# Loading order in a fused linear-attention and expert kernel: reciprocals read back in two halves, wo loaded inside the loop, x tiles on other queues

## The chip, the cores and the metric

The kernel runs on one core of a Trainium2 chip. The core has five engines that run side by side and wait for each other through semaphores: TensorE (PE, with its weight loads PEld), VectorE (DVE), ScalarE (ACT), GpSimd (POOL) and SyncE (SP). SP only issues DMAs here; ScalarE and GpSimd issue a few too. The metric is device time in microseconds (us) for one execution. The kernel before takes 110.32 us, the median of 3 runs (109.84 to 110.73).

## The reference

The input x is one sequence of S = 2048 tokens of D = 640. It is normalised to xn, and three things are added: x, a linear attention of 32 heads on xn, and a small expert block on xn that changes 8 tokens only.

```python
def _A_ref(x, wqkv, wo):                       # on xn
    qkv = (x @ wqkv) ...                       # q, k, v in 32 heads of 20
    phi = lambda t: jnp.where(t > 0, t + 1, jnp.exp(t)) + 1e-6
    pq, pk = phi(q), phi(k)
    kv = jnp.einsum("bhsd,bhse->bhde", pk, v)
    z = jnp.einsum("bhsd->bhd", pk)
    num = jnp.einsum("bhqd,bhde->bhqe", pq, kv)
    den = jnp.einsum("bhqd,bhd->bhq", pq, z)[..., None] + 1e-6
    return (num / den) ... @ wo

def _B_ref(x, w_r, w_gate, w_up, w_down):      # on xn
    r = x @ w_r
    idx = jnp.argsort(-r, axis=-1)[:, :8]      # 8 tokens
    y = (silu(x_sel @ w_gate) * (x_sel @ w_up)) @ w_down * sigmoid(r_sel)
    return x + scatter_add(y at idx)

xn = layernorm(x)
return x + _A_ref(xn, A_wqkv, A_wo) + _B_ref(xn, ...)
```

All inputs and the output are bf16.

## The kernel before

**Tiles.** The tokens are 16 tiles of 128 (T = 16); D is five chunks of 128 (KC = 5, the index m or kc). Everything stays in the core's memory: x_sb and xn hold tokens in rows, xnT, pqT and rb hold features in rows and tokens in columns.

**Order.** The order of the instructions on each engine is written out by hand (manual_schedule); each engine works through its own list strictly in that order. Waits between engines are put in by the framework. DMAs take eight completion semaphores in turn, and a DMA that takes one over waits until the DMA that had it before has landed. SP's DMAs therefore stand in one queue, in program order, and a DMA that waits holds up those behind it.

**Start (lines 108 to 118).** SP and ScalarE read x tiles, wk (the k columns of wqkv, in two parts: chunks 0 to 2 and 3 to 4) and wq. Tile 0 comes in two halves of 320 columns, tile 1 whole on SP (L111), tile 2 on SP (L114), tile 3 on ScalarE (L115), tiles 4 to 7 in one DMA on SP (L118). VectorE takes the statistics of each tile (ln_stats, L165), GpSimd the root, VectorE normalises (ln_norm, L193). The first three tiles are transposed on TensorE, later ones by a DMA transpose on SP (L198) into xnT.

**Loop over tiles (L437 to L471).** For tile t, TensorE multiplies k (L240, needs xnT of t), the Gram matrix of xn with phi(k) of tile t - 1 (ga_mm, L263, tiles gaC and gaD) and q (L252). ScalarE and VectorE turn q and k into phi(q) = pqT and phi(k) = pk. In each round late_loads(t) lets SP issue one of the remaining loads: x tiles 8 to 15, wg, wu, wd and wv, by a table. From t = 12 keep(...) copies x + xn to a scratch in DRAM (xcp, L390).

**Between loop and output.** Column sums of pk go through zpart and four tiny DMAs (zrel, L522) to give z; late_loads(16) then loads wo, in two DMAs (L380, L381). TensorE goes on with the Gram matrix (gb1, L533; gb2, L630), multiplies the denominators (pden, L611), and the gate and up projections of the 8 tokens (L643). ScalarE takes the reciprocals as exp(-ln den), rden, laid out as 4 groups of 32 heads by 512 tokens.

**Reciprocals (L656 to L683).** rden has heads in rows, but pqT has features in rows. So four stores on SP (rscr_store, one for each 512 tokens) write it to a DRAM scratch rscr, and rb_load(a, b) reads tokens a to b back, each head's row spread over its features: five DMAs, one for each m. The first call takes SP and ScalarE in turn, the others SP alone. norm(a, b) on VectorE then multiplies pqT by rb for tiles a to b; norm(0, 2) needs the five DMAs that bring tokens 0 to 511, norm(8, 12) and norm(12, 16) those of the last 1024 tokens.

**Output.** GT, the whole Gram matrix, times wv gives kvT (L708, L715), kvT times wo gives M in five chunks (m_chunk, L743; copied out by ScalarE and once by VectorE, L754). In VectorE's list stand, in this order: kvT, norm(0, 2), y_sb (the copy of the 8 tokens' result py, L774), M's chunk 3, norm(2, 4), norm(4, 8), norm(8, 12), norm(12, 16), the additions. M's chunk 4 is multiplied into the same buffer that py had. y_sb is scattered onto xcp by GpSimd (L775), and x_sb is read back from there (L780). o_mm(t) (L795) multiplies pqT by M for tile t; x_sb is added, and the tile is written out.

Of the kernel before, what the change touches and what calls it, by code (L numbers as in the profile page):

```python
# [9 lines left out]
S = 2048  # L10
D = 640
# [3 lines left out]
T = S // P  # L15
KC = D // P
FC = F // P
C = 8
TBLK = 512
NTB = S // TBLK  # L20
HW = 320
# [4 lines left out]
E0 = (0, 80, 180, 280, 380, 480, 512)  # L26
# [21 lines left out]
def kernel(  # L48
# [13 lines left out]
    nc = tc.nc  # L62
# [4 lines left out]
    x_v = A_x[0].rearrange("(t p) d -> p t d", p=P)  # L67
# [8 lines left out]
    def sb(shape, dt, name, tag=None):  # L76
        return big.tile(shape, dt, tag=tag or name, name=name)
# [7 lines left out]
    x_sb = sb([P, T, D], BF16, "x_sb")  # L85
# [6 lines left out]
    wv = sb([P, KC, D], BF16, "wv")  # L92
    wo = sb([P, NW, D], BF16, "wo")
# [14 lines left out]
    nc.gpsimd.dma_start(wrow[:], B_w_r.rearrange("(kc p) -> kc p", p=P))  # L108
    nc.sync.dma_start(x_sb[:, 0, 0:HW], x_v[:, 0, 0:HW])
    nc.scalar.dma_start(x_sb[:, 0, HW:D], x_v[:, 0, HW:D])  # L110
    nc.sync.dma_start(x_sb[:, 1, :], x_v[:, 1, :])  # L111
    nc.scalar.dma_start(wk[:, 0:3, 0:D], wqkv_v[:, 0:3, D : 2 * D])
    nc.sync.dma_start(wk[:, 3:KC, 0:D], wqkv_v[:, 3:KC, D : 2 * D])
    nc.sync.dma_start(x_sb[:, 2, :], x_v[:, 2, :])  # L114
    nc.scalar.dma_start(x_sb[:, 3, :], x_v[:, 3, :])  # L115
    for a, b in ((0, 3), (3, KC)):
        nc.sync.dma_start(wq[:, a:b, :], wqkv_v[:, a:b, 0:D])
    nc.sync.dma_start(x_sb[:, 4:8, :], x_v[:, 4:8, :])  # L118


    zero = sb([P, P], BF16, "zero")
# [236 lines left out]
    def wo_rows(a, stride, n):  # L358
        return bass.AP(
            tensor=A_wo.tensor, offset=A_wo.offset + a * D,  # L360
            ap=[[D, P], [stride * D, n], [1, D]],
        )

    def late_loads(t):
        def part(dst, src, a, b):
            nc.sync.dma_start(dst[:, a:b, :], src[:, a:b, :])

        wv_v = wqkv_v[:, :, 2 * D : 3 * D]
        plan = {
            2: (x_sb, x_v, 8, 12), 4: (wg, kcF, 0, 1), 5: (x_sb, x_v, 12, 16),  # L370
            6: (wg, kcF, 1, 3), 7: (wg, kcF, 3, 5), 8: (wu, kcU, 0, 2), 9: (wu, kcU, 2, 4),
            10: (wu, kcU, 4, 5), 11: (wd, kcD, 3, 8), 12: (wd, kcD, 8, FC), 13: (wv, wv_v, 0, 2),
            14: (wv, wv_v, 2, KC),
        }
        if t in plan:
            part(*plan[t])
        if t == 10:
            part(wd, kcD, 0, 3)
        if t == 16:
            nc.sync.dma_start(wo[:, 0::6, :], wo_rows(E0[0], E0[6], 2))  # L380
            nc.sync.dma_start(wo[:, 1:6, :], wo_rows(E0[1], 100, 5))  # L381

    gaC = pair("C", "gaC")
    gaD = bank("D0", "gaD")
# [52 lines left out]
    for t in range(2, T):  # L437
# [27 lines left out]
        if 11 < t < T - 1:  # L465
            for u in range(4 * (t - 12) + 4, 4 * (t - 12) + 7):
                residual(u)
        small_consts(t)
        late_loads(t)
        if t > 11:  # L470
            keep(4 * (t - 12), 4 * (t - 11))  # L471
# [48 lines left out]
    with nc.allow_non_contiguous_dma(reason="column sums from rows to partitions"):  # L520
        for i in range(4):
            (nc.sync, nc.scalar)[i % 2].dma_start(  # L522
                zrel[:, i, :], zpart[32 * i : 32 * i + 1, :].rearrange("o (p m) -> o p m", m=KC)
            )
    late_loads(T)
    nc.scalar.copy(GT[:, 0:2, 0:TBLK], two(gaC[:]))
    nc.scalar.copy(GT[:, 2, 0:TBLK], gaD[:])

# [136 lines left out]
    def rb_load(a, b, engs=(nc.sync,)):  # L665
        src = rscr[:, a:b].rearrange("(m s) n -> s m n", m=KC)
        for m in range(KC):
            engs[m % len(engs)].dma_start(
                rb[:, m, a:b], src[:, m, :].unsqueeze(1).to_broadcast([P // 4, 4, b - a])
            )  # L670
# [3 lines left out]
    for t in range(DEN_AT, T):  # L674
        gb1(t)
    nc.scalar.copy(GT[:, 3:5, 0:TBLK], two(gbA[:]))
    rb_load(0, TBLK, (nc.sync, nc.scalar))
    rb_load(TBLK, 2 * TBLK)
    rb_load(2 * TBLK, S)

    def norm(a, b):
        sl = pqT[:, :, a * P : b * P]
# [80 lines left out]
    for fc in range(FC):  # L763
        j, b = fc // 3, fc % 3
# [59 lines left out]
    for t in range(NPRE, T):  # L824
# [6 lines left out]
        else:  # L831
            for i in range(3):
                a, b = LAST[i : i + 2]
# [7 lines left out]
def two(ap):  # L841
    return ap.rearrange("p (b f) -> p b f", b=2)
# [30 lines left out]
```

## Time and profile before

| | |
|---|---|
| median of 3 runs | 110.32 us (109.84 to 110.73) |
| the profiled execution | 109.81 us, its span 108.0 us |
| granted TensorE clock | 1.000 |
| TensorE busy | 102.8 us (95% of the span) |
| VectorE busy | 79.9 us (74%) |
| ScalarE busy | 66.4 us (61%) |
| GpSimd busy | 35.4 us (33%) |
| DMA | 25.64 MB, mean 237 GB/s, most of it on SP's queue (q1) |

How to read it: times are from the start of the span, the first to the last instruction. A timeline row has start, duration, engine, line, operation, output and inputs. A row of the chain has start and duration of a piece of the chain of work that ended last. A row of a line's own view has the operation, durations in ns (min/median/max), and the first and last start; its DMA line has the time from issue to landing. A row of a stretch (from:to) has its length, the busy time of PE, PEld, DVE, ACT and POOL (with the number of instructions), the granted clock, the busy share of the DMA engines and their GB/s. A DMA queue's row has packets, MB and the share of the 16 DMA engines' time.

### The profile page before, as it was taken

How to read it: one execution, taken by the hardware profiler on the slowest of the kernel's cores; microseconds unless marked ns; L12 is line 12 of the kernel's file. 1: busy time of each engine (PE TensorE's matmuls, PEld its weight loads, DVE VectorE, ACT ScalarE, POOL GpSimd, SP SyncE). 2: the span in 40 equal slices, each digit the busy share in tenths (PEclk: the TensorE clock that was granted, in tenths of full speed). 3: DMA queues.
4: the chain of work that ended last, by engine and by line, in shares of the span. 5: the costliest groups of instructions: out<-in, count | busy, mean ns of one | idle time of the engine just before them, and what ended most of it. 6: DMA issues, size and time to landing. Idle time of an engine off the chain costs nothing.

```text
span 108.0 us, 2937 instructions
## 1 busy us (share of the span) xinstructions
PE 102.8 (95%) x1132; PEld 68.4 (63%) x1146; DVE 79.9 (74%) x200; ACT 66.4 (61%) x119; POOL 35.4 (33%) x81
## 2 busy tenths in 40 slices
PE   6999999999999999999999999999999999999980
PEld 2547867776677766777677744456996555555550
DVE  3879999979999799987999886814038705938670
ACT  4358977779777797778877855469029455555000
POOL 5423096988897757681000000210003300000000
PEclk9999999999999999999999999999999999999999
DMA  2999053995597999999999991685674798999883
GB/s 67 299 377 345 13 61 61 259 99 155 90 285 154 245 331 204 370 367 187 318 352 394 389 393 53 140 294 116 193 235 150 233 304 262 276 311 393 313 289 122
DMA packets 27406, 25.64 MB, mean 237 GB/s; under 512 B 10880, under 2 KB 25472, under 8 KB 27392
## 3 DMA queue, kind: packets, MB, share of 16 engines
q1 hardware_dynamic: 25232, 23.70, 76.8%
q10 hardware_dynamic: 1984, 1.71, 4.8%
q0 software_dynamic: 176, 0.04, 0.6%
q8 instruction: 9, 0.15, 0.5%
q14 instruction: 5, 0.04, 0.2%
HBM read 17.37 MB, written 5.94 MB: 216 GB/s over the span
## 4 chain that ended last, share of the span: by engine, by line
PE 84%; DVE 9%; DMA 2%; issue 1%; POOL 1%; DVEq 0%
PE q L252 19%; PE k L240 18%; PE o L795 14%; PE gbA L533 6%; PE gaC L263 6%; PE gbC L630 4%; PE gaD L263 3%; DVE st L165 3%; DMA x_sb<-in_A_x_dram 2%; PE gu L643 2%; DVE xn L193 1%; DVE o_all L803 1%; PE pkv L708 1%; PE M L743 1%; PE zp L503 1%
## 5 line engine op out<-in xcount | busy, mean ns | idle before, releaser
L252 PEld LDWEIGHTS <-wq 128*128 128x128 bf16 x400 | 23.6, 98 | 3.6
L240 PE MATMUL k<-wk,xnT 128*128 128x129 bf16 (+1 forms) x152 | 24.5, 296 | 0.5
L252 PE MATMUL q<-xnT,wq 128*128 128x128 bf16 x400 | 25.0, 219 | 0.0
L795 PEld LDWEIGHTS <-pqT 128*128 128x128 bf16 x165 | 12.7, 98 | 9.3 <-issue 0.3
L215 ACT ACTIVATE eq<-q 128x640 bf16<-128x640 f32 x16 | 11.2, 703 | 10.2 <-PE q L252 10.1
L240 PEld LDWEIGHTS <-xnT 128*128 128x128 bf16 x160 | 12.3, 98 | 8.0 <-ACT xnT L208 0.5
L795 PE MATMUL o<-M,pqT 128*128 128x128 bf16 (+1 forms) x108 | 15.7, 298 | 0.1
L165 DVE BATCH_NORM_STATS2 st<-x_sb 128x6 f32<-128x320 bf16 x32 | 14.1, 478 | 1.0 <-DMA x_sb<-in_A_x_dram 1.0
L227 DVE SCALAR_TENSOR_TENSOR pk<-ek,rk 128x640 bf16<-128x640 bf16 x16 | 13.2, 824 | 2.2 <-ACT rk L218 1.7
L178 POOL TENSOR_TENSOR sq<-sq,half 128x1 bf16<-128x1 bf16 x16 | 12.4, 772 | 6.3 <-DVE sq L173 3.2
L227 DVE SCALAR_TENSOR_TENSOR pqT<-eq,rq 128x640 bf16<-128x640 bf16 x16 | 13.1, 818 | 0.2 <-ACT rq L218 0.2
L215 ACT ACTIVATE ek<-k 128x640 bf16<-128x640 f32 x16 | 11.2, 703 | 1.7 <-DVE r_all L441 0.3
L218 ACT ACTIVATE rq<-q 128x640 bf16<-128x640 f32 x16 | 11.2, 700 | 0.0
L218 ACT ACTIVATE rk<-k 128x640 bf16<-128x640 f32 x16 | 11.2, 698 | 0.0
L819 ACT CAST o_all<-o 128x640 bf16<-128x640 f32 x9 | 6.2, 692 | 6.1 <-PE o L795 6.1
L180 POOL TENSOR_TENSOR sc<-sq,neg 128x1 f32<-128x1 bf16 x12 | 9.0, 754 | 0.9
L683 DVE TENSOR_TENSOR pqT<-pqT,rb 128x2560 bf16<-128x2560 bf16 (+1 forms) x5 | 6.0, 1222 | 4.5 <-DMA rb<-rscr 4.4
L263 PE MATMUL gaC<-pk,xn 128*128 128x512 bf16 x31 | 9.3, 377 | 0.1
L581 POOL COPY xsT<-xnT 128x5 bf16 x8 | 1.2, 222 | 20.5 <-DVE zc L583 20.5
L193 DVE TENSOR_SCALAR xn<-x_sb,sc 128x640 bf16<-128x640 bf16 (+2 forms) x17 | 6.9, 410 | 1.0 <-POOL sc L181 0.8
L533 PE MATMUL gbA<-pk,xn 128*128 128x512 bf16 x30 | 7.2, 380 | 0.2 <-issue 0.2
L387 DVE TENSOR_TENSOR x_sb<-x_sb,xn 128x640 bf16<-128x640 bf16 x16 | 7.2, 484 | 0.0
(155 smaller groups left out, 121.7 us busy)
## 6 DMA issues: line engine op xcount, KB each, us to landing
xcp<-x_sb SPq DMA_DIRECT2D x4, 640.0 KB, 7.4
x_sb<-in_A_x_dram SPq DMA_DIRECT2D x3, 640.0 KB, 4.6
x_sb<-xcp SPq DMA_DIRECT2D x3, 640.0 KB, 8.4
out_dram<-o_all SPq DMA_DIRECT2D x11, 160.0 KB, 5.1
wg<-in_B_w_gate_dram SPq DMA_DIRECT2D x2, 768.0 KB, 6.1
wu<-in_B_w_up_dram SPq DMA_DIRECT2D x2, 768.0 KB, 6.8
rb<-rscr SPq DMA_DIRECT2D x5, 256.0 KB, 4.7
rb<-rscr SPq DMA_DIRECT2D x8, 128.0 KB, 3.4
```

The source lines that it names most:

```text
L165: nc.vector.bn_stats(out=stat[t][:, h, :], in_=x_sb[:, t, h * HW : (h + 1) * HW])
L178: nc.gpsimd.tensor_tensor(out=sq[:, 1:2], in0=sq[:, 0:1], in1=half[:], op=ALU.pow)
L180: nc.gpsimd.tensor_tensor(out=sc[:, 1:2], in0=sq[:, 1:2], in1=neg1[:], op=ALU.pow)
L193: nc.vector.tensor_scalar(out=xn[:, t, a:b], in0=x_sb[:, t, a:b], scalar1=sc[:, 0:1], scalar2=sc[:, 1:2], op0=ALU.subtract, op1=ALU.mult,)
L215: nc.scalar.activation(e[:], ps[:, 0:D], AF.Exp)
L218: nc.scalar.activation(r[:], ps[:, 0:D], AF.Relu)
L227: nc.vector.scalar_tensor_tensor(out=dst, in0=ea, scalar=1.0, in1=ra, op0=ALU.min, op1=ALU.add)
L240: nc.tensor.matmul(ps[:, a:b], lhsT=xnT[:, kc, t * P : (t + 1) * P], rhs=wk[:, kc, a:b], start=(kc == 0), stop=(kc == KC - 1),)
L252: nc.tensor.matmul(ps[:, m * P : (m + 1) * P], lhsT=wq[:, kc, m * P : (m + 1) * P], rhs=xnT[:, kc, t * P : (t + 1) * P], start=(kc == 0 an ...
L263: nc.tensor.matmul(gaC[:, c * TBLK : (c + 1) * TBLK] if c < 2 else gaD[:], lhsT=xn[:, t, c * P : (c + 1) * P], rhs=pk[:, t, 0:TBLK], start ...
L533: nc.tensor.matmul(gbA[:, (c - 3) * TBLK : (c - 2) * TBLK], lhsT=xn[:, t, c * P : (c + 1) * P], rhs=pk[:, t, 0:TBLK], start=(t == 0), stop ...
L795: nc.tensor.matmul(ps, lhsT=pqT[:, m, t * P : (t + 1) * P], rhs=M[:, m, a:b], start=(m == M_ORDER[0]), stop=(m == M_ORDER[-1]),)
```

## The change

Four edits to the loading, none to the arithmetic:

- x tile 1 is read in two halves, on SP and ScalarE; tile 3 is read by SP behind tile 2, not by ScalarE; tiles 4 to 7 come in two DMAs of two tiles.
- wo is loaded in four parts from late_loads: its blocks 1 and 2 at t = 3, 3 to 5 at t = 4, 0 and 6 at t = 15. The call after the column sums is gone.
- wv's second part (chunks 2 to 4) is split: 2 and 3 at t = 14, 4 at t = 15.
- rb is read in two calls of 1024 tokens, in place of 512, 512 and 1024. The first call uses SP and ScalarE in turn.

```diff
     nc.sync.dma_start(x_sb[:, 0, 0:HW], x_v[:, 0, 0:HW])
     nc.scalar.dma_start(x_sb[:, 0, HW:D], x_v[:, 0, HW:D])
-    nc.sync.dma_start(x_sb[:, 1, :], x_v[:, 1, :])
+    nc.sync.dma_start(x_sb[:, 1, 0:HW], x_v[:, 1, 0:HW])
+    nc.scalar.dma_start(x_sb[:, 1, HW:D], x_v[:, 1, HW:D])
     nc.scalar.dma_start(wk[:, 0:3, 0:D], wqkv_v[:, 0:3, D : 2 * D])
     nc.sync.dma_start(wk[:, 3:KC, 0:D], wqkv_v[:, 3:KC, D : 2 * D])
-    nc.sync.dma_start(x_sb[:, 2, :], x_v[:, 2, :])
-    nc.scalar.dma_start(x_sb[:, 3, :], x_v[:, 3, :])
+    for t in (2, 3):
+        nc.sync.dma_start(x_sb[:, t, :], x_v[:, t, :])
     for a, b in ((0, 3), (3, KC)):
         nc.sync.dma_start(wq[:, a:b, :], wqkv_v[:, a:b, 0:D])
-    nc.sync.dma_start(x_sb[:, 4:8, :], x_v[:, 4:8, :])
+    for t in (4, 6):
+        nc.sync.dma_start(x_sb[:, t : t + 2, :], x_v[:, t : t + 2, :])
...
-            14: (wv, wv_v, 2, KC),
+            14: (wv, wv_v, 2, 4), 15: (wv, wv_v, 4, KC),
...
-        if t == 16:
-            nc.sync.dma_start(wo[:, 0::6, :], wo_rows(E0[0], E0[6], 2))
-            nc.sync.dma_start(wo[:, 1:6, :], wo_rows(E0[1], 100, 5))
+        for a, b in {3: ((1, 3),), 4: ((3, 6),), 15: ((0, 1), (6, 7))}.get(t, ()):
+            nc.sync.dma_start(wo[:, a:b, :], wo_rows(E0[a], E0[2] - E0[1], b - a))
...
-    late_loads(T)
...
-    rb_load(0, TBLK, (nc.sync, nc.scalar))
-    rb_load(TBLK, 2 * TBLK)
-    rb_load(2 * TBLK, S)
+    rb_load(0, S // 2, (nc.sync, nc.scalar))
+    rb_load(S // 2, S)
```

Line numbers move by two at the start and are one less from L660 on (the multiplication by rb is L683 before and L682 after).

## The prediction

> **What bounds the kernel now.** The page's first two sections and its chain come first.
>
> ```profile
> PE 102.8 (95%) x1132; PEld 68.4 (63%) x1146; DVE 79.9 (74%) x200; ACT 66.4 (61%) x119; POOL 35.4 (33%) x81
> PE 84%; DVE 9%; DMA 2%; issue 1%; POOL 1%; DVEq 0%
> ```
>
> TensorE is busy for 102.8 of 108.0 us, and the chain that ends last is matmuls for 84%, with DMA for 2% and unexplained issue for 1%. So a transfer can only matter where it makes TensorE wait, or where the chain is not TensorE. The chain in order of time shows those places:
>
> ```profile
> 0.80 2.23 DMA x_sb<-in_A_x_dram
> ...
> 4.43 0.82 DVE st L165 x2
> ...
> 7.62 0.89 DVE st L165 x2
> ...
> 11.75 0.59 PE gaC L263 x2
> ...
> 27.66 0.27 PE k L240 x2
> ...
> 31.09 1.38 PE k L240 x10
> ...
> 69.95 1.19 PE pden L611 x20
> ...
> 82.41 0.61 PE M L743 x16
> ...
> 102.15 1.37 PE o L795 x10
> ```
>
> The chain begins with the landing of the first part of x, 2.23 us, which is its only DMA (2% of the span). Up to 11.75 us it is then mostly VectorE's statistics and normalisation, and from there to 102.15 + 1.37 = 103.5 us matmul after matmul. Nothing in the middle can become much faster by loading earlier; it can become slower.
>
> **Part 1, the start.** Tile 1 of x is read in two halves, on SP and ScalarE; its second half stands ahead of wk's first part on ScalarE's queue; tile 3 moves to SP behind tile 2; tiles 4 to 8 come in two DMAs. SP issues two DMAs more than before, ScalarE as many. Timeline rows, and the landings of tile 2 (L114), then of wk's first part (L112):
>
> ```profile
> 4.36 0.37 SPq L118 DMA_DIRECT2D x_sb<-in_A_x_dram  x1
> ...
> 6.61 1.25 PE L240 MATMUL k<-wk,xnT 128*128 128x512 bf16 x5
> ...
> 12.17 0.88 DVE L165 BATCH_NORM_STATS2 st<-x_sb 128x6 f32<-128x320 bf16 x2
> ...
> L114 SPq DMA_DIRECT2D x_sb<-in_A_x_dram x1: 470/470/470, 2.2 to 2.2; - x1
> ...
> DMA to landing us min/median/max: 5.4/5.4/5.4
> ...
> L112 ACTq DMA_DIRECT2D wk<-in_A_wqkv_dram x1: 457/457/457, 1.3 to 1.3; - x1
> ...
> DMA to landing us min/median/max: 4.5/4.5/4.5
> ```
>
> SP's DMA of L118 waits for tile 1 and goes at 4.36, so tile 1 is there by then; VectorE reaches its statistics at 4.43 in the chain, straight from the work before. Tile 2 lands at 2.2 + 5.4 = 7.6, and its statistics follow tile 1's normalisation without a gap at 7.62. Earlier landings gain nothing in this execution: 0. They give tile 2 a margin, since it now has 80 KB less ahead of it on SP. wk's first part lands at 1.3 + 4.5 = 5.8; 80 KB more ahead, at its own 480 KB in 4.5 us, make it 0.75 later at most: 6.55, still before the matmul at 6.61. Tiles 4 to 8 now wait for wk's second part instead of tile 1, but stand in the queue behind wq anyway and are wanted at 12.17. I cost the start at 0, between a gain of 0.3 (an execution in which tile 2 is late) and a loss of 0.2.
>
> **Part 2, wo inside the loop.** 320 KB go out after tile 5's transpose, 480 KB behind wg's first part, 320 KB ahead of the last copy of x to scratch. On SP's queue the transposes that feed the k matmuls stand behind them. SP's sixth, of tile 6, then that of tile 7, and the load of SP's own DMA queue around them:
>
> ```profile
> L198 SPq DMA_TRANSPOSE xnT<-xn x1: 1200/1200/1200, 22.3 to 22.3; - x1
> ...
> DMA to landing us min/median/max: 3.8/3.8/3.8
> ...
> L198 SPq DMA_TRANSPOSE xnT<-xn x1: 1206/1206/1206, 26.2 to 26.2; - x1
> ...
> DMA to landing us min/median/max: 2.7/2.7/2.7
> ...
> q1 hardware_dynamic: 1588, 0.85, 69.8%
> ```
>
> Tile 6 lands at 26.1, 1.6 us before k(6) at 27.66; tile 7 at 28.9, 2.2 before k(7) at 31.09. The last row is SP's queue from 22.5 to 30 us: 69.8% busy, 2.3 us free. The 800 KB (0.82 MB) need 2.2 us at the 371 GB/s that the row of 87.40 to 88.00, below, reaches. The first 320 KB (0.88) stay inside tile 6's margin, and all of it would just eat tile 7's if nothing fell in the gaps. Cost 0; upper end, at half that rate and no gap, 2.2 x 2 - 2.2 = 2.2 us. Of wv the fifth chunk moves behind the next copy of x, nothing waits for it there.
>
> The last 320 KB push the copy of tiles 12 to 16 back by 0.9, and the column sums zrel stand behind it on SP:
>
> ```profile
> 53.00:65.00 12.00, 11.85 (x146) 7.84 (x145) 10.99 (x28) 8.87 (x16) 0.00 (x0) 1.00 1.08 379
> ...
> L522 SPq DMA_DIRECT2D zrel<-zpart x1: 826/826/826, 66.5 to 66.5; - x1
> ...
> 69.42 0.33 DVE L587 TENSOR_TENSOR zm<-headm,zc 128x160 bf16<-128x160 bf16 x1
> ```
>
> The DMA engines are full up to 65 (share 1.08); if that copy's data end soon after, 0.9 later is some 66, still before zrel's issue at 66.5. zm is ready at 69.75, 0.2 ahead of pden. Cost 0, with 0.5 as the upper end. wo's old place is after zrel (L380, L381), and its readers, the M matmuls, have no DMA wait in the chain, so vacating it gains 0.
>
> **Part 3, the reciprocals.** rden goes to scratch in four stores of 512 tokens, and rb is read back, five DMAs (one per m) for each stretch. Before: 512, 512, 1024 tokens, 15 DMAs of 128, 128 and 256 KB. After: 1024 and 1024, ten of 256 KB. The first normalisation needs all five of the first stretch. So it now needs twice the bytes, and the first read waits for the second store too. The second store and all stores' landing, the old first, fifth, eleventh and last reads (each with its landing), the rates, and VectorE:
>
> ```profile
> L660 SPq DMA_DIRECT2D rscr<-rden x1: 609/609/609, 73.3 to 73.3; - x1
> ...
> DMA to landing us min/median/max: 2.7/2.8/3.0
> ...
> 75.38 0.56 SPq L668 DMA_DIRECT2D rb<-rscr  x1
> ...
> DMA to landing us min/median/max: 2.7/3.4/4.2
> ...
> L668 SPq DMA_DIRECT2D rb<-rscr x1: 629/629/629, 76.6 to 76.6; - x1
> ...
> DMA to landing us min/median/max: 4.5/4.5/4.5
> ...
> L668 SPq DMA_DIRECT2D rb<-rscr x1: 602/602/602, 82.7 to 82.7; - x1
> ...
> DMA to landing us min/median/max: 4.0/4.0/4.0
> ...
> L668 SPq DMA_DIRECT2D rb<-rscr x1: 1347/1347/1347, 85.6 to 85.6; - x1
> ...
> DMA to landing us min/median/max: 4.6/4.6/4.6
> ...
> 84.40:85.60 1.20, 1.20 (x11) 0.64 (x9) 0.57 (x1) 0.69 (x1) 0.17 (x1) 1.00 0.79 271
> 87.40:88.00 0.60, 0.60 (x7) 0.32 (x5) 0.00 (x0) 0.54 (x1) 0.00 (x0) 1.00 1.05 371
> ...
> 81.26 0.82 DVE L683 TENSOR_TENSOR pqT<-pqT,rb 128x1280 bf16<-128x1280 bf16 x1
> ...
> 82.19 0.32 DVE L774 CAST y_sb<-py 128x160 bf16<-128x160 f32 x1
> ```
>
> Before, the first read went at 75.38 and landed 2.7 later, at 78.1; the last of its five at 76.6 + 4.5 = 81.1. VectorE's multiplication began at 81.26, so it had nothing to spare. After:
>
> - The second store goes at 73.3 and lands 2.8 later, 76.1; the first read goes then, not at 75.38: 0.8 later.
> - It lands 2.7 later, plus 0.35 for its second 128 KB at 371 GB/s: 79.2.
> - Four more of 256 KB follow. Pace per DMA: 0.71 us at 371 GB/s, 0.97 at 271. The old third stretch, of the same size, landed its first at 82.7 + 4.0 = 86.7 and its fifth at 85.6 + 4.6 = 90.2: 0.89 each. I take that, the same DMA on the same queue: 79.2 + 4 x 0.89 = 82.75. The ends: 82.0 and 83.1; above them, by bytes at the old first stretch's pace of (81.1 - 78.1) / 4 = 0.75 per 128 KB, 79.2 + 4 x 1.5 = 85.2; below them 81.6, worked out with the first rival.
>
> Behind the multiplication on VectorE are the cast of y (82.19) and then the copy of M's fourth chunk. The matmuls of the fifth chunk use y's buffer, so they wait for that cast, which ended at 82.51, some 0.2 before TensorE came to them (its 32 small matmuls of 82.41 to 83.02, second half). Hence TensorE stands for 82.75 - 81.2 - 0.2 = **1.35 us**, with the ends from 0.6 to 1.7, at the outside 0.2 and 3.8.
>
> Given back: the multiplications of tokens 512 to 1024 and 1024 to 2048 no longer wait (these waits hung nothing, o(8) being far off), five DMAs less are issued, and y's scatter and the reload of x run with less beside them. The scatter starts late by the same 1.35, and the end is TensorE's last ten matmuls at 102.15 and the additions after them; all of this shifts and gains 0.
>
> **Sum.** 0 + 0 + 1.35. The profiled execution took 109.81 us (span 108.0, 1.8 around it): 111.2. It lies 0.5 under the median of the runs, 110.32; on that median 1.35 gives **111.7**, 1.2% more. What a measurement of this kernel can tell from no change is about 1%, 1.1 us.
>
> **A rule against it.** The old first stretch, 640 KB, took 5.7 us from first issue to last landing. The Trainium skill, "DMA: Bandwidth & Descriptors", section "Anatomy of one DMA — SWDGE (gpsimd) path", fits a DMA by about 2 us plus its bytes at 436 GB/s, which makes fewer, larger DMAs the cheaper ones. By it the 1280 KB would be there an estimated 2.0 + 3.0 us after 76.1, at 81.1, and TensorE would not wait: 110.3. For 640 KB it would say 3.5 where the rows have 5.7; the measurement decides, and what the rule would bring is the first rival.
>
> **The rivals.**
> - *Hidden, no change*: with 256 KB pieces the five overlap on two queues and the DMA engines run full. A landing without its data costs 2.0 us (the 2.23 of the chain's first row less 80 KB at 371 GB/s), the 1.31 MB 3.5: 76.1 + 5.5 = 81.6, where TensorE begins to wait at 81.4. For it: the 371 of 87.40; against it: 271 at 84.40. Time 110.5.
> - *The loop stalls as well*: wo's 800 KB find no gaps, tile 7's transpose passes 31.09, or zrel is so late that zm passes 69.95. It decides from 2.2 us of delay in the loop or 0.2 at zrel, and its price lies between 0 and the 2.2 of part 2; I take 0.9. For it: both transposes have little room. Against it: the 2.3 us free. On top of 111.7: 112.6.
> - *Faster*: the start's margins, 7.6 against 7.62, are so thin that the usual execution, 0.5 over the profiled one, loses time there; tile 2's earlier landing then gives some of it back, and the reciprocals are hidden. 109.9 or less; faster by over 1% only with more than that.
>
> **How the numbers follow.** Late reciprocals 0.66, of which 0.43 above 1% (a stall over 1.1 us) and 0.23 below; hidden 0.14; loop as well 0.12; start relieved 0.08, of which 0.05 counts as faster by over 1%. Slower: 0.43 + 0.12 = 0.55, with a little for what I don't see 0.57; within 1%: 0.23 + 0.14 + 0.01; faster 0.05. The range goes from 110.2 (leaving out the start and part of the hidden case) to 113.0 (a stall of 2.7; the far end of 3.8 stays out).
>
> **What would show it.** The multiplication L682 near 82.8 instead of 81.26, with its wait ended by rb; a gap of TensorE over 1 us between M's chunks or ahead of o(0); the first rb landing near 79.2 and the fifth near 82.75. Parts 1 and 2 are right if gaC starts near 11.75 and pden near 69.95. I am wrong if rb's fifth read lands before 81.4, or if TensorE has gaps at the k matmuls.

## The result and the profile after

The changed kernel takes **117.47 us**, the median of 6 runs (116.05 to 118.99), against 110.11 (109.84 to 111.35) for the kernel before on the same chip: a ratio of 1.057, 95% interval 1.047 to 1.066. The forecast of 111.7 (110.2 to 113.0) was right in sign and far too small. The profiled execution after took 117.03 us, 7.2 more than the one before (109.81).

The comparisons leave out executions over 1.5% above the fastest of their kernel; in this case some of these are executions in which TensorE's clock fell once more, so the medians below, which hold all executions, stand beside the ratios.

The page of the kernel after: TensorE's busy time, the clock granted to it in 40 slices of the span, and the shares of the chain that ended last.

```profile
PE 104.0 (90%) x1132; PEld 69.0 (60%) x1146; DVE 80.0 (69%) x200; ACT 66.5 (58%) x119; POOL 36.0 (31%) x81
...
PEclk9975599999999999999999999999999999999999
...
PE 75%; DMA 16%; DVE 2%; ACT 2%; issue 1%; SPq 1%; ACTq 0%; DVEq 0%
```

TensorE's share of the span went from 95% to 90%, DMA's share of the chain from 2% to 16%, and the clock row has a dent (7, 5, 5) in its third to fifth slices. The chain of the kernel after in order of time (start, duration, piece) shows the two places:

```profile
1.74 7.40 DMA wk<-in_A_wqkv_dram
...
9.28 2.29 PE k L242 x5
...
16.50 0.43 PE gaC L265 x2
...
74.54 1.22 PE pden L611 x20
...
80.90 4.29 DMA rb<-rscr
...
85.21 3.78 DMA rb<-rscr
...
90.57 0.38 PE o L794 x2
```

Set beside the chain of before, three amounts come out:

- *The start.* The first matmul of k began at 6.61; it now waits for wk's first part and begins at 9.28: **+2.67**. wk's first part was issued at 1.26 and landed 4.5 later, at 5.74; now ScalarE issues it at 1.74, behind the half tile, and it takes 7.40 and lands at 9.14.
- *The clock.* The first five matmuls of k took 1.25 and take 2.29, and gaC begins at 16.50 instead of 11.75, 4.75 later. So another **2.1** is lost after k has begun.
- *The reciprocals.* pden is 4.59 late (74.54 against 69.95): the loop gave back 0.16 and lost nothing. The first matmul of o, which followed M at 82.41 + 0.61 = 83.02, comes at 90.57, 7.55 late: **+2.96** between pden and o.

4.59 and 2.96 make 7.55, of which 0.3 is given back by the end. The clock is that of this row of the view by stretches (length, busy time of PE, PEld, DVE, ACT, POOL, the granted clock, the DMA engines' share, GB/s), after:

```profile
7.40:14.15 6.75, 4.87 (x22) 2.68 (x23) 3.01 (x13) 1.91 (x5) 0.55 (x1) 0.50 0.63 216
```

For 6.8 us the granted clock is 0.50; the trace has it at full speed before (3.94 to 7.36) and after. TensorE had nothing to do for 2.8 us ahead of k. The timelines of VectorE and TensorE after show the second place:

```profile
89.00 0.82 DVE L682 TENSOR_TENSOR pqT<-pqT,rb 128x1280 bf16<-128x1280 bf16 x1 [3.19 <-DMA rb<-rscr]
...
90.11 0.46 PE L742 MATMUL M<-wo,kvT 128*32 128x512 bf16 x8 [2.84 <-DVE y_sb L773]
```

The wait is where the forecast put it (VectorE for rb, and behind it M's last chunk for y's copy), but 2.84 us long and not 1.35. A DMA here is spread over 16 DMA engines and counts as landed when all 16 have finished. The trace has each engine's end, and for the fifth read of the first stretch it says: 15 engines from 86.67 to 87.27, the sixteenth at 88.78. Among these reads, at 86.21, a 16 KB fetch of TensorE's own instructions ran on one DMA engine for 0.97 us. Both the start and this fetch had to be tested.

### The profile page after: what moved, and what is told of

The parts are those of the page before. It is cut to its first block, busy times and chain, and to the rows that moved or that the text cites. A ratio compares the mean times of both kernels' runs of the same rounds, so it can differ in the third digit from the quotient of the medians.

```text
span 115.3 us, 2936 instructions
## 1 busy us (share of the span) xinstructions
PE 104.0 (90%) x1132; PEld 69.0 (60%) x1146; DVE 80.0 (69%) x200; ACT 66.5 (58%) x119; POOL 36.0 (31%) x81
## 4 chain that ended last, share of the span: by engine, by line
PE 75%; DMA 16%; DVE 2%; ACT 2%; issue 1%; SPq 1%; ACTq 0%; DVEq 0%
PE k L242 21%; PE q L254 19%; PE o L794 13%; DMA rb<-rscr 7%; DMA wk<-in_A_wqkv_dram 6%; PE gaC L265 6%; PE gbA L533 5%; PE gaD L265 3%; DMA rscr<-rden 2%; DVE o_all L802 1%; PE pden L611 1%; PE zp L504 1%; PE o13a L794 1%; PE o9a L794 1%; PE o1a L794 1%
## 5 line engine op out<-in xcount | busy, mean ns | idle before, releaser
L242 PE MATMUL k<-wk,xnT 128*128 128x129 bf16 (+1 forms) x152 | 26.4, 314 | 3.2 <-DMA wk<-in_A_wqkv_dram 2.8
L242 PEld LDWEIGHTS <-xnT 128*128 128x128 bf16 x160 | 13.2, 103 | 11.4 <-issue 4.2
L820 DVE TENSOR_TENSOR o_all<-o_all,x_sb 128x640 bf16<-128x640 bf16 x12 | 5.4, 490 | 7.1 <-DMA x_sb<-xcp 4.6
L182 POOL TENSOR_TENSOR sc<-sq,neg 128x1 f32<-128x1 bf16 x12 | 9.7, 812 | 0.9
L682 DVE TENSOR_TENSOR pqT<-pqT,rb 128x2560 bf16<-128x2560 bf16 (+1 forms) x5 | 5.8, 1219 | 3.2 <-DMA rb<-rscr 3.2
```

The source lines that it names most:

```text
L182: nc.gpsimd.tensor_tensor(out=sc[:, 1:2], in0=sq[:, 1:2], in1=neg1[:], op=ALU.pow)
L242: nc.tensor.matmul(ps[:, a:b], lhsT=xnT[:, kc, t * P : (t + 1) * P], rhs=wk[:, kc, a:b], start=(kc == 0), stop=(kc == KC - 1),)
```

## The experiments

All edits but the last are made to the kernel before. Times are medians with lowest and highest; the profiled execution is one of them.

### Which part costs what

**All edits of the start, nothing else.**

> The kernel before with the start's edits alone (x tile 1 in halves on two queues, tile 3 on SP behind tile 2, tiles 4 to 7 in two DMAs). Theory A, the parts add up: in the changed kernel wk's first part landed 3.4 us later and TensorE's chain was 4.7 us late at gaC, so 110.1 + 4.7 = 114.8, with gaC near 16.5. Rival B, the loss at the start needs no edit of the start's order but is chance of one execution: 110 to 111, gaC near 11.8. My prediction's step said 0, 110.1.

```diff
-    nc.sync.dma_start(x_sb[:, 1, :], x_v[:, 1, :])
+    nc.sync.dma_start(x_sb[:, 1, 0:HW], x_v[:, 1, 0:HW])
+    nc.scalar.dma_start(x_sb[:, 1, HW:D], x_v[:, 1, HW:D])
...
-    nc.scalar.dma_start(x_sb[:, 3, :], x_v[:, 3, :])
+    nc.sync.dma_start(x_sb[:, 3, :], x_v[:, 3, :])
...
-    nc.sync.dma_start(x_sb[:, 4:8, :], x_v[:, 4:8, :])
+    for t in (4, 6):
+        nc.sync.dma_start(x_sb[:, t : t + 2, :], x_v[:, t : t + 2, :])
```

Measured: 112.35 (110.36 to 114.22; before 110.05). No two of the four executions agree: 110.36, 111.35, 113.36, 114.22. Neither forecast holds: the median lies between A's 114.8 and the 110 to 111 of B. The profiled execution was the fastest; its chain:

```profile
1.74 5.30 DMA wk<-in_A_wqkv_dram
...
7.18 1.24 PE k L242 x5
```

wk's first part lands at 7.04 and not at 9.14, k takes its usual 1.24, the clock never falls. So the loss of the start changes from one execution to the next, from 0.3 to 4.2 us, and one profile does not tell its size.

**wo (and wv's split) alone.**

> The kernel before with wo in four parts inside the loop and wv's split alone. Theory A (TensorE without a gap from gaC to pden in the changed kernel): no change, 110.1 within 0.5. Rival B: the loop's transposes or the column sums come late once the start no longer gives them time: 110.6 to 112.

```diff
-            14: (wv, wv_v, 2, KC),
+            14: (wv, wv_v, 2, 4), 15: (wv, wv_v, 4, KC),
...
-        if t == 16:
-            nc.sync.dma_start(wo[:, 0::6, :], wo_rows(E0[0], E0[6], 2))
-            nc.sync.dma_start(wo[:, 1:6, :], wo_rows(E0[1], 100, 5))
+        for a, b in {3: ((1, 3),), 4: ((3, 6),), 15: ((0, 1), (6, 7))}.get(t, ()):
+            nc.sync.dma_start(wo[:, a:b, :], wo_rows(E0[a], E0[2] - E0[1], b - a))
...
-    late_loads(T)
```

Measured: 110.53 (109.94 to 112.01; before 110.05), ratio 1.004 (1.000 to 1.009). Its chain has gaC, pden and o where before has them (11.75, 69.95, 83.02):

```profile
11.74 0.56 PE gaC L263 x2
...
69.90 1.19 PE pden L609 x20
...
82.98 1.14 PE o L793 x7
```

No loss that can be measured. The profiled execution was the slowest of the nine (112.01), and what it lost came behind the last matmul: from there to the end of the span it took 5.4 us, before 3.1. On the last writes of the output the sixteenth DMA engine landed 1.0 us behind the other 15. The clock fell to half at 107.85, 2.9 us after the last matmul.

**The reciprocals in two halves alone.**

> The kernel before with the reciprocals in two halves alone. Theory A, the parts add up: 110.1 + 2.9 = 113.0; the fifth read of the first half lands near 84.2, 3.0 later than before. Theory C, the pace alone (0.89 us for each 256 KB) makes it late and the rest of the 2.9 came from one DMA engine that was held up by a fetch of instructions in that execution: 111.5 (1.35 more) where the fetch falls elsewhere, 113.0 where it falls there again. Rival B, hidden: 110.1.

```diff
-    rb_load(0, TBLK, (nc.sync, nc.scalar))
-    rb_load(TBLK, 2 * TBLK)
-    rb_load(2 * TBLK, S)
+    rb_load(0, S // 2, (nc.sync, nc.scalar))
+    rb_load(S // 2, S)
```

Measured: 113.92 (112.74 to 114.83; before 110.05), so 3.9 over before and not the prediction's 1.35. The four executions fall in two pairs by the mean granted clock: 112.74 and 113.20 at 1.00, 114.64 and 114.83 at 0.985. The chain of the profiled one (113.20):

```profile
77.45 7.22 DMA rb<-rscr
...
84.79 0.82 DVE pqT L682
...
85.90 0.46 PE M L742 x8
86.36 1.47 PE o L794 x10
```

The first read went at 76.20 and landed at 79.11, as forecast (76.1 and 79.2). But the fifth took 7.22 and landed at 84.67, not at 82.75. Fifteen engines had it by 82.74, the figure forecast; the sixteenth came at 84.67. The fetch had begun at 81.48, among the reads, where theory C has 113.0; the median is 0.9 over that.

**Tile 1's halves alone.**

> The kernel before with x tile 1 in halves on SP and ScalarE alone; tile 3 stays on ScalarE, tiles 4 to 7 in one DMA. Theory A1, the half tile ahead of wk's first part on ScalarE's queue makes wk late: 114 to 115, as with all edits of the start. Theory A2, it is tile 3 on SP and the rest that crowds SP's queue, while the half costs 0.5 at most: 110.1 to 110.6.

```diff
-    nc.sync.dma_start(x_sb[:, 1, :], x_v[:, 1, :])
+    nc.sync.dma_start(x_sb[:, 1, 0:HW], x_v[:, 1, 0:HW])
+    nc.scalar.dma_start(x_sb[:, 1, HW:D], x_v[:, 1, HW:D])
```

Measured: 113.3 (113.04 to 114.94; before 110.05), ratio 1.029 (1.025 to 1.032). The median lies under the 114 to 115 of theory A1, but far over A2's 110.6; two of the six executions (114.78 and 114.94) lie in A1's range. The chain of the profiled execution (114.94) repeats that of the whole change:

```profile
1.74 7.14 DMA wk<-in_A_wqkv_dram
...
9.02 2.29 PE k L241 x5
...
16.60 0.43 PE gaC L264 x2
```

**Tiles 3 to 7 alone, tile 1 whole.**

> Tile 1 stays whole on SP; only tile 3 goes behind tile 2 on SP and tiles 4 to 7 go in two transfers. Theory (the loss of the start belongs to tile 1's halves alone): wk's first part lands near 5.7 as before, gaC starts near 11.75, time 110.1 (109.7 to 110.7). Rival (a longer SP queue behind wk's second part takes share from wk's first part too): it lands at 6.5 or later and the time is over 111.

```diff
-    nc.scalar.dma_start(x_sb[:, 3, :], x_v[:, 3, :])
+    nc.sync.dma_start(x_sb[:, 3, :], x_v[:, 3, :])
...
-    nc.sync.dma_start(x_sb[:, 4:8, :], x_v[:, 4:8, :])
+    for t in (4, 6):
+        nc.sync.dma_start(x_sb[:, t : t + 2, :], x_v[:, t : t + 2, :])
```

Measured: 110.64 (109.76 to 115.61; before 110.53), ratio 1.001 (0.997 to 1.006). k at 6.73 and gaC at 11.86 in its chain. One execution of ten took 115.61; it was not the one profiled, and what happened in it is open. wk's first part lands at 5.40. The start's loss belongs to tile 1's halves.

### Why the halves make wk late

**wk's first part ahead of the second half.**

> Tile 1 in halves, the second half issued on ACT's queue behind wk's first part instead of ahead of it; nothing else. Theory A (the 82 KB ahead of wk's first part, which let wk's second part on SP catch up with it, make it late): wk's first part lands near 5.7 as before; the second half lands behind it, near 6.2, VectorE's statistics of tile 1 and behind them the normalisation of tile 0 wait for it, and the first matmul of k starts near 7.8 instead of 6.6; time 111.3, gaC near 13. Rival B (any second small transfer of x, or two rings that read wk side by side, slows the reads whatever their order): wk's first part lands at 7 to 9 and the time is 112.5 to 114.

```diff
     nc.scalar.dma_start(x_sb[:, 0, HW:D], x_v[:, 0, HW:D])
-    nc.sync.dma_start(x_sb[:, 1, :], x_v[:, 1, :])
+    nc.sync.dma_start(x_sb[:, 1, 0:HW], x_v[:, 1, 0:HW])
     nc.scalar.dma_start(wk[:, 0:3, 0:D], wqkv_v[:, 0:3, D : 2 * D])
+    nc.scalar.dma_start(x_sb[:, 1, HW:D], x_v[:, 1, HW:D])
```

Measured: 113.22 (113.05 to 113.70), ratio 1.026 (1.020 to 1.031). Its chain now begins with x and not with wk:

```profile
1.74 5.09 DMA x_sb<-in_A_x_dram
...
8.60 2.28 PE k L241 x5
...
15.24 0.43 PE gaC L264 x2
```

wk's first part is there by 5.71, as before (5.74): theory A. The second half of tile 1 lands at 6.83, VectorE's normalisation of tile 0 waits for it, and k begins at 8.60; the forecast for this was 7.8. Of the 1.9 that the time lies over its forecast, 0.8 is this; the rest fits the clock, which fell here too, for 3.4 us (k takes 2.28 and not 1.25). The time alone (113.22) lies in B's range of 112.5 to 114; the landing decides.

**Tile 2 ahead of wk's second part on SP.**

> Tile 1 in halves on both queues as in the change; on SP tile 2 is issued ahead of wk's second part, so that wk's first part on ACT runs beside x rows and not beside wk's own rows. Theory A (what makes wk's first part late is that both rings read wk's rows at the same time from the start): it lands at 6 to 6.5, wk's second part near 8, for which the fourth matmul of k waits; gaC 13, time 111 to 111.8. Rival B (it shares bandwidth with whatever SP reads): it lands at 7 to 9 as with the halves alone, time 112.5 to 114.

```diff
+    nc.sync.dma_start(x_sb[:, 2, :], x_v[:, 2, :])
     nc.sync.dma_start(wk[:, 3:KC, 0:D], wqkv_v[:, 3:KC, D : 2 * D])
-    nc.sync.dma_start(x_sb[:, 2, :], x_v[:, 2, :])
```

(beside tile 1's halves). Measured: 113.79 (112.46 to 114.21), ratio 1.023 (1.014 to 1.031).

```profile
1.74 6.67 DMA wk<-in_A_wqkv_dram
...
8.54 1.24 PE k L241 x5
...
13.62 0.43 PE gaC L264 x2
```

wk's first part is late (8.41) beside rows of x too, not only beside wk's own: rival B in the landing and the time. This run also gives the price of the clock. k begins at 8.54, as with the edit before (8.60), but at full clock; gaC follows 5.08 later, there 6.64 later. One stretch of half clock costs 1.6 here.

**Everything behind the halves on one queue.**

> Tile 1 in halves on both queues as in the change, but everything behind them (wk's two parts, tiles 2 and 3, wq, tiles 4 to 7) is issued on ACT's queue in one order; SP's queue carries only the first halves of tiles 0 and 1. Theory A (wk's first part is late because it shares the 16 DMA engines with what SP's queue reads at the same time): with nothing beside it, it lands at 5.6 to 6.5 although the same 82 KB stand ahead of it, and wk's second part follows near 7.2. Rival B (the small transfer ahead of it and the slow first packets make it late whatever SP reads): it lands at 7 or later. The time is muddied, since ACT issues longer before its first copy, on which TensorE's mask and transposes wait: by A k starts at 6.6 to 7.6 and the time is 110.2 to 111.5, by B it is 112.5 or above.

```diff
-    nc.sync.dma_start(wk[:, 3:KC, 0:D], wqkv_v[:, 3:KC, D : 2 * D])
-    nc.sync.dma_start(x_sb[:, 2, :], x_v[:, 2, :])
+    nc.scalar.dma_start(wk[:, 3:KC, 0:D], wqkv_v[:, 3:KC, D : 2 * D])
+    nc.scalar.dma_start(x_sb[:, 2, :], x_v[:, 2, :])
...
-        nc.sync.dma_start(wq[:, a:b, :], wqkv_v[:, a:b, 0:D])
-    nc.sync.dma_start(x_sb[:, 4:8, :], x_v[:, 4:8, :])
+        nc.scalar.dma_start(wq[:, a:b, :], wqkv_v[:, a:b, 0:D])
+    nc.scalar.dma_start(x_sb[:, 4:8, :], x_v[:, 4:8, :])
```

(beside tile 1's halves). Measured: 112.62 (111.54 to 113.96), ratio 1.015 (1.005 to 1.025); wk's first part lands at 6.84, between the two forecasts, and the time, which is B's, says little: TensorE waited for ScalarE's late first copy (1.5) and later for rb (0.9), not for wk. The DMA view of 3.2 to 5.7 us compares the two causes. Rows: busy tenths of the 16 DMA engines in 40 slices (a packet counts in the slice in which it starts), packets and rate, then the queues (q10 is ScalarE's, q1 SP's) with packets, MB and share of the engines' time. Before:

```profile
DMA  1756369787999999999999998999999998998999
...
DMA packets 714, 0.84 MB, mean 335 GB/s; under 512 B 61, under 2 KB 714, under 8 KB 714
...
q10 hardware_dynamic: 459, 0.57, 64.9%
q1 hardware_dynamic: 223, 0.27, 30.8%
```

After:

```profile
DMA  9995000492355974968699979997767778979799
...
DMA packets 476, 0.56 MB, mean 222 GB/s; under 512 B 34, under 2 KB 476, under 8 KB 476
...
q1 hardware_dynamic: 229, 0.28, 45.2%
q10 hardware_dynamic: 229, 0.28, 33.2%
```

All on ScalarE's queue:

```profile
DMA  5990011595296764667979989999989999989899
...
DMA packets 535, 0.63 MB, mean 250 GB/s; under 512 B 43, under 2 KB 535, under 8 KB 535
...
q10 hardware_dynamic: 512, 0.62, 85.1%
```

Before, the queue that reads wk's first part moved 0.57 MB in these 2.5 us; after, 0.28. Two causes offer themselves. One is the share: SP finishes its small half sooner and reads wk's second part and tile 2 beside it, so that after, each queue moves 229 packets. The other is the rate, 222 and 250 against 335: behind the small halves no new packet starts around 3.5 us (the zeros in both rows) and only 7 to 11 are under way, by the packets' own times, where before, with tile 1 still to move, 15 were.

How much belongs to which is not shown. Without a neighbour the part landed at 6.84, with one at 9.14 (the whole change), 9.11, 8.88 and 8.41, but at 7.04 in the fastest execution of the start's edits, where SP read beside it as well. What goes with the landing there is the rate: 290 GB/s in the same stretch, against 222 to 259 in the late ones. Nor does a neighbour suffice: with wk ahead of the half it had one, at 350 GB/s, and landed at 5.71. So the order is shown as the cause, and the slow restart behind the halves and the share are how it probably works. Why the reads restart slowly stays open; single packets of 1280 bytes took up to 0.9 us, but so did one before (0.86).

**Dummy matmuls over the wait.**

> Tile 1 in halves as in the change, the rest as before, and 7 dummy matmuls of 512 columns between the transposes of tile 0 and the first matmul of k, 1.5 us that keep TensorE busy while it waits for wk's first part. Theory A (half of the start's loss is the clock, which falls to half speed after the idle stretch): wk's first part lands at 7 to 9.1 as with the halves alone, k starts at 8.1 to 9.3, the clock stays full, gaC starts at 13.2 to 14.4 and the time is 111.6 to 112.8, with the high values of the halves alone (114 to 115) gone. Rival B (the clock costs nothing, the late landing alone): gaC as with the halves alone, near 16.5 where wk lands near 9, and a time of 113.3 or above.

```diff
+    warm_mm(TBLK, 7)
     kp = k_mm(0, "A", transposes_1)
```

(beside tile 1's halves). Measured: 113.40 (112.69 to 114.15), ratio 1.031 (1.022 to 1.040).

```profile
1.74 7.37 DMA wk<-in_A_wqkv_dram
...
9.24 1.24 PE k L241 x5
...
14.32 0.43 PE gaC L264 x2
```

Theory A's mechanism is confirmed: wk lands at 9.11, as late as ever, k begins at 9.24, the clock stays full, and gaC begins at 14.32 where the whole change with the same landing has 16.50. The forecast of the time, 111.6 to 112.8, failed. In this execution TensorE also stood 0.6 for y's copy, behind a read of rb whose sixteenth engine came 1.4 late (84.56 against 83.16) behind a fetch of instructions at 82.35, although rb was in its old three stretches. The dummies would also cost time where wk lands early, which no trace here shows. The median is no better than with the halves alone (113.3).

### What holds the reciprocals back

**The fetch moved forward.**

> Reciprocals in two halves, wo and the start as before; the 8 dummy matmuls of 512 columns at the start become 43 of 56 columns, which puts 70 more instructions (a matmul and its weight load each) ahead on TensorE and so moves the places at which its instructions are fetched (16 KB on one DMA engine, about every 250 instructions). Theory A (the fetch in the midst of the first five reads holds one of the 16 DMA engines back and with it the landing): without a fetch between 77.5 and 82.7 all 16 engines are there by 82.8, the first norm starts near 82.9 and the first matmul of o near 84.4; time 111.5 (111.1 to 112). Rival B (the bytes of the larger reads and their wait for the second store alone): the norm starts at 84.8 as with the halves alone, time 113.5 to 114.5. If the fetch still falls among the reads, the run says nothing between the two.

```diff
-    warm_mm(TBLK, WARM)
+    warm_mm(56, 43)
```

(beside rb in two halves). Measured: 114.87 (113.92 to 117.32), ratio 1.033 (1.026 to 1.039). The fetch moved, from 81.5 to 79.4, but still lay at the beginning of the reads, so by its own words the run does not decide by the time; its start was disturbed as well (tile 1 landed late and the clock fell for 3.4 us). What it shows is that the lag moved along with the fetch:

| run | fetch of 16 KB | read | 15 engines done | the sixteenth |
|---|---|---|---|---|
| halves alone | 81.48 | first | 79.11 (all 16) | |
| halves alone | | fifth | 82.74 | 84.67 |
| fetch moved | 79.38 | first | 81.64 | 83.39 |
| fetch moved | | fifth | 85.22 | 86.67 |
| the whole change | 86.21 | first | 83.67 (all 16) | |
| the whole change | | fifth | 87.27 | 88.78 |

**The fetch out of the way.**

> Reciprocals in two halves as in the change, the rest as before, and the second column block of G (gb2) left out: its five matmuls of 128 columns for each tile become two of 512 and 128, of other operands, so that TensorE is busy for as long with 96 instructions fewer, and the fetch of its instructions that fell among the first five reads (at 81.5 with the halves alone) comes later or among other bytes. The output is not the reference's in these columns. Theory A (the fetch holds one of 16 DMA engines back): with no fetch from 77.5 to 82.5 all 16 engines are there near 82.8, the first norm starts at 82.8 to 83.1, the first matmul of o near 84.5; time 111.6 (111.2 to 112.2). Rival B (bytes and the second store's wait alone make the loss): norm near 84.8, time 113.5 to 114.5. If a fetch falls among the reads at another place, the sixteenth engine lags from that place on, as theory A says, and the time lies between.

```diff
-        for c in range(KC):
+        for c, (a, z) in enumerate(((0, TBLK), (TBLK, D))):
             nc.tensor.matmul(
-                gbC[:, c * P : (c + 1) * P],
+                gbC[:, a:z],
                 lhsT=xn[:, t, c * P : (c + 1) * P],
-                rhs=pk[:, t, TBLK:D],
-                start=(t == 0 and c in (0, 4)), stop=(t == T - 1),
+                rhs=pk[:, t, a:z],
+                start=(t == 0), stop=(t == T - 1),
```

(beside rb in two halves). Measured: 111.41 (111.39 to 112.77; before 110.10), ratio 1.016 (1.007 to 1.025). Its chain:

```profile
77.42 5.50 DMA rb<-rscr
...
83.04 0.83 DVE pqT L682
...
84.15 0.46 PE M L742 x8
```

The fetch came at 83.6, after the fifth read had landed on all 16 engines at 82.92. The normalisation starts at 83.04 (forecast 82.8 to 83.1), TensorE waits 1.6 instead of 3.3. Against the halves alone at full clock (112.74 and 113.20) the median is 1.3 to 1.8 lower, and the two executions with a lower mean clock (114.64, 114.83) have no counterpart. Theory A. The rows of the DMA queues from 77.5 us to the fifth read's end make the difference plain; the instruction fetch is q8. First the halves alone, 77.5 to 82.7:

```profile
q1 hardware_dynamic: 584, 1.08, 57.9%
q10 hardware_dynamic: 281, 0.51, 30.4%
q8 instruction: 1, 0.02, 1.1%
```

The same with the fetch out of the way, 77.5 to 82.9:

```profile
q1 hardware_dynamic: 570, 1.05, 57.1%
q10 hardware_dynamic: 288, 0.52, 35.9%
```

One packet among 866 decides the landing. The traces of all fourteen kernels bear it out: of the rb reads whose 16 ends a trace gives, the sixteenth engine is at first 0 to 0.5 us behind the fifteenth; then, beginning with a read whose other 15 engines finish 0.4 to 2.3 us after the fetch began, 0.8 to 1.9. In the kernel before, that is a read of tokens 512 to 1023, for which TensorE did not wait.

### Do the parts add up

**The whole change, tile 1 whole.**

> The whole change but tile 1's halves: tile 1 whole on SP as before. Theory (the start's loss is the halves' alone, the rest of the loss is the reciprocals', and the two add up): gaC near 11.75, pden near 69.9, norm near 84.8, time 113.9 (113 to 114.8). Rival (the parts need each other, wo in the loop or tile 3's place cost together what they do not alone): over 115.

Against the changed kernel:

```diff
-    nc.sync.dma_start(x_sb[:, 1, 0:HW], x_v[:, 1, 0:HW])
-    nc.scalar.dma_start(x_sb[:, 1, HW:D], x_v[:, 1, HW:D])
+    nc.sync.dma_start(x_sb[:, 1, :], x_v[:, 1, :])
```

Measured: 115.01 (113.18 to 115.73; before 110.10), ratio 1.034 (1.023 to 1.045). The median lies a little above the forecast of 113.9 (113 to 114.8) and, by 0.01, above the rival's bound of 115, so by the time alone the rival is not out. But gaC, pden and the multiplication by rb are where the theory has them (11.68, 69.86, 84.89), and the execution at full clock, 113.18, is like those of the reciprocals alone (112.74 and 113.20). What is more in the profiled one is the clock again. Waits of TensorE in the profiled execution (115.73), then the granted clock:

```profile
PE M L741 <- DVE y_sb L772: 3.3, 1, 3.3
```

```profile
84.90:91.65 6.75, 5.43 (x26) 2.59 (x27) 6.72 (x7) 1.38 (x2) 1.75 (x1) 0.50 0.34 74
```

The clock fell during the wait for rb as well, for 6.8 us, and the matmuls of o behind it took twice as long (a pair of o1a and o1b every 0.53 us; with the fetch out of the way every 0.27). With the reciprocals alone TensorE waited as long for rb, 3.3, and the clock stayed full. In every trace the changes of the clock lie a whole multiple of 3.41 us apart, so each execution can be laid out in windows of that length. The windows that hold the wait, first here, then with the reciprocals alone (the first figure behind the length is TensorE's busy time):

```profile
81.44:84.86 3.42, 1.23 (x56) 0.88 (x45) 0.00 (x0) 1.67 (x4) 0.00 (x0) 1.00 1.06 386
```

```profile
80.59:84.00 3.41, 2.00 (x80) 1.44 (x78) 0.52 (x1) 2.04 (x4) 0.00 (x0) 1.00 1.02 385
84.00:87.42 3.42, 1.52 (x17) 0.78 (x17) 2.63 (x5) 0.69 (x1) 1.27 (x1) 1.00 0.49 167
```

Here most of the wait lies in one window and the clock falls at its end, at 84.86; there it is split over two. But the busy time of a window does not decide by itself: in the whole change the clock fell behind a window with 1.73 us (3.94 to 7.35) and not behind one with 1.41 (85.86 to 89.27). What else counts is open.

Ahead of the last matmul the traces have half clock for 3.4 us or twice that. 3.4 of 111 us at half is 0.015 of the mean granted clock, so the mean, which every execution has, hints at how often it happened:

| kernel | clock 1.00 | 0.985 | 0.970 | 0.956 |
|---|---|---|---|---|
| rb in halves | 112.74, 113.20 | 114.64, 114.83 | | |
| change, tile 1 whole | 113.18 | 114.50 | 115.52, 115.73 | |
| the whole change | | 116.05 | 116.65, 117.03, 117.90 | 118.88, 118.99 |

From one column to the next the times rise by 0.6 to 2.3 us; 3.4 us at half speed would be 1.7 if TensorE were always busy. But the mean is not a count. With tile 2 ahead of wk's second part it was 0.986 although the clock was full up to 109.17, 2.5 us after the last matmul: this execution, like the profiled one of wo alone, ended late (5.6 and 5.4 us from the last matmul to the end, 2.9 to 3.4 in the other twelve traces), the sixteenth engine again 1.0 behind on the last writes, and the half clock lay in that idle end. Such an end costs some 2 us and lowers the mean as one stretch does. So the two stretches are shown for the profiled executions of the whole change (117.03) and of this one (115.73); for the others, the 114.64 and 114.83 of the reciprocals alone among them, it can't be told how much is a fallen clock and how much a late end. The kernel before stood between 0.98 and 1.00, nearly always at 0.99 or above.

No part gained time, alone or with the others.

## Why the prediction was wrong

**Part 1, the start, cost 0: wrong, by most of the loss.** The step that failed is "80 KB more ahead ... make it 0.75 later at most", worked out from wk's own 480 KB in 4.5 us. Two things were wrong in it. It left out that ScalarE issues wk's first part behind the half tile, 0.48 later (1.74 against 1.26); with the 0.75 that makes 1.23, more than the margin of 0.87 (5.74 against 6.61), and it is close to the best landings with the halves (7.04 and 6.84, so 1.3 and 1.1 later). And it took the queue's rate as given, while the halves changed the rate (335 to 222 GB/s from 3.2 to 5.7 us) and the share (65% to 33% of the engines' time): in the profiled execution the part landed 3.4 later. That tile 2 would get a margin was wrong as well: it landed at 8.97 instead of 7.59. What held is that tiles 3 to 7 cost nothing where tile 1 stayed whole.

On this the Trainium skill, "DMA: Bandwidth & Descriptors", section "Issuing engines are not separate DMA queues", says that DMAs issued by different engines run on the same 16 DMA engines and interleave, so that a second issuing engine saves little but issue time. The rows of q1 and q10 agree (45.2% and 33.2% of the same engines' time), and reading tile 1 by two queues brought it in earlier (3.76; before, SP's DMA that waits for it went at 4.36) but gained no time.

**A term that was not in the sum: the clock.** The granted clock was 1.000 before, and the sum had no step for what a gap of TensorE does to it. A wait of 2.8 us ahead of k cost another 2.1; with the dummies in the wait k began as late, the clock stayed full and gaC came 2.2 earlier. The Trainium skill, "TensorE: Matmul & The Clock Gate", Part 1, says that the clock halves after an idle window of about 3.4 us, that the windows run freely, whatever the kernel does, and that a busy window brings it back. The lengths agree (3.41 and 6.83 us at 0.50). The threshold doesn't: waits of 2.8, 2.5, 2.3 and 1.9 us ahead of k or of the transposes before it were followed by half clock, another of 1.9 was not; of the waits for rb, one of 3.3 was, another of 3.3, one of 3.1 and one of 2.8 were not. TensorE was busy for 32% to 51% of the windows after which the clock fell, so none of them was idle throughout. That it depends on where the gap falls among the windows fits the changes of the clock at multiples of 3.41 us, and would explain part of the 2 us by which executions of one kernel differ; which gap is long enough was not tested.

**Part 2, wo, cost 0: right.** Alone it measured 1.004 (1.000 to 1.009), and pden had no delay of its own with wo in the loop.

**Part 3, 1.35: right in place and mechanism, too small by a term.** With the fetch out of the way it is right in its numbers too: the first landing 79.25 against 79.2, the fifth 82.92 against 82.75, TensorE's wait 1.64 against 1.35, the time 1.3 over before by the medians. The pace of 0.89 a DMA held on average (3.67 / 4 = 0.92), though the landings come at uneven distances. What failed is that the landing was taken as bytes at a pace: it is the end of the slowest of 16 engines. A fetch of instructions held one of them back, by 1.9 with the reciprocals alone and by 1.5 in the whole change. The kernel before has such a fetch too, at 80.67, only 0.5 before its last needed landing: that it cost nothing there was luck. In two of the four executions alone another 1.4 to 2.1 came on top, at a lower mean clock, for which the cause is not shown. The outside bound of 3.8 covers TensorE's wait of 3.3, for another reason than the pace that it was worked out from.

**The rivals.** *Hidden* fell with the fifth landing: 82.92 even with the fetch out of the way, not 81.6; the rule's 81.1 fell with it. *The loop stalls as well* fell with wo alone. *Faster*, by tile 2's earlier landing, was the reverse of the truth: the profiled execution of before had tile 2 at 7.59, just in time; after, it landed at 8.97, and VectorE waited 1.4 for it, which k's delay hid.

**What would show it.** The text named a gap at the k matmuls and a gaC later than 11.75 as signs against part 1; both came.

The loss up to o by its terms, in the profiled execution: 2.67 for the landing, 2.08 for the clock, 0.16 back; of the 2.96 of the reciprocals 1.5 for the sixteenth engine, so that 1.45 is left where 1.35 was forecast.

## What to carry to other kernels

A margin under 1 us between a landing and its reader at the start of a kernel is no margin against a change in what stands on the queues: splitting a tile to have it earlier delays the issue of what comes behind and can change its share and rate. When a wait is put ahead of TensorE, its price is the wait and what the clock then takes; look at the granted clock in the trace, where it fell and for how long, and at more than one execution, since the mean alone also counts an idle end. And read a landing engine by engine: a wait for one large batch of DMAs is a wait for the slowest of 16 engines, and what holds that one back can be another queue's single packet. A smaller first batch stands less long in its way, but is not safe: with the dummies the old one of 512 tokens was caught too.

## What was not expected of the hardware

- A 16 KB instruction fetch on one DMA engine, 0.95 us long, made the landing of the reads around it 0.8 to 1.9 us later than on the other 15, in each of the fourteen traces. TensorE's longest wait that nothing in these traces explains is 0.2 us. The fetch recurs about every 250 instructions of TensorE (2278 matmuls and weight loads, 9 fetches), so adding or removing matmuls far away moves it into or out of a critical transfer. The Trainium skill, "Runtime: NRT & Kernel Launch", section "Instruction fetch mechanics", has the blocks of 16 KiB and 256 instructions and calls their cost mostly hidden; the trace agrees on size and distance (9 packets of q8, 0.15 MB), and shows where the cost is not hidden. Why 0.95 us of fetch becomes up to 1.9 us of lag is open.
- The granted clock fell to 0.50 in or after gaps of 1.9 to 3.3 us, for 3.4 or 6.8 us, but not after each of them, and always at a multiple of 3.41 us from its other changes.
- 80 KB ahead of a 480 KB read on one queue, with or without another queue's reads beside it, made it land 1.1 to 3.4 us later, by another amount in each profiled execution.
- In two of the fourteen traces the last writes of the output landed 1.0 us later on one of the 16 DMA engines than on the others, and the execution ended some 2 us late.
